# Top-k attention with a SwiGLU block on one core: transposes, scores and sums over V moved between the turns of a software pipeline

## The chip, the core and the metric

The kernel runs on one core of a Trainium2 chip. A core has five engines that run side by side, each with its own queue that it works off in order: TensorE (PE in the profile, PEld for its weight loads), VectorE (DVE), ScalarE (ACT), GpSimd (POOL) and SyncE (SP, which issues most of the DMAs). They wait for each other only through semaphores. TensorE writes into PSUM, from which ScalarE or VectorE copies (evicts) a result into SBUF. The metric is the device time of one execution in microseconds (us).

## What is computed

```python
def _attn_ref(q, k, v):                      # 8 batches, 8 heads, 576 tokens, 64 wide
    scores = scale * np.matmul(q, k.transpose(0, 1, 3, 2))
    kth = np.partition(scores, -top_k, axis=-1)[..., -top_k:-top_k + 1]   # top_k = 32
    scores = np.where(scores >= kth, scores, -1000000000.0)
    attn = np.exp(scores - np.max(scores, axis=-1, keepdims=True))
    attn = attn / (np.sum(attn, axis=-1, keepdims=True) + 1e-09)
    return np.matmul(attn, v).astype(np.float32)

def _moe_ref(x, w_gate, w_val, w_out):       # x is 4608 x 512, w_* 512 x 1536 and 1536 x 512
    g = x @ w_gate
    silu = g * (1.0 / (1.0 + np.exp(-g)))
    return (silu * (x @ w_val) @ w_out).astype(np.float32)
```

The attention's output, with the heads side by side, is the x of the second block. All is float32.

## The kernel before

**Units.** The attention is cut into 160 units: a batch, a tile of 128 queries and a pair of heads. Of the 20 units of a batch, 16 hold two heads of 128 queries ("full" units); the last 4 hold the remaining 64 queries, both heads side by side in one 128-row tile ("J units", `qt == J` in the code), with half the selecting to do. A unit goes through these steps:

- `scores` (line 288): TensorE multiplies Q by K, 4 matmuls into 4 PSUM banks (8 smaller ones for two J units at once); ScalarE evicts them to `sc` (L330, or L315 for J units).
- `select` (333): VectorE finds the 32 largest of each row, four rounds of MAX8 (L347) with three of MATCH_REPLACE8 between (L351), for each head. `shift` (357): GpSimd forms the bias of the exponential (L362).
- `weigh` (367): ScalarE applies Prelu (L374), which sends what is below the 32nd value far down, and exp with a running sum (L379).
- `normalize` (387): VectorE takes the reciprocal of the sum (L392, L393); then ScalarE multiplies head 0 of `e` by it (L397) and GpSimd head 1 (L399; both heads for the first 12 units).
- `turn` (403): TensorE transposes `e` in 128x128 blocks, 9 for a full unit (L412): four that lie in head 0, one that lies across both heads, four in head 1. ScalarE copies them to `et` (L413).
- `values` (423): TensorE sums over V for two units at once, 40 small matmuls in the trace's records for each pair (L448); ScalarE copies the result to `xT` (L465), from which the second block is fed.

PSUM tiles of these steps (`s`, `etps`, `av`, `kqps`) come from one pool of 5 banks, given out in turn; those of the second block from another of 3.

**The second block** (FFN) is cut into blocks of 256 tokens and these into pieces, which the generator `feed` (587) hands out one at a time. A piece is 4 matmuls by `wg` or `wv` (L604; each is two records in the trace), and two pieces make one tile. When a tile is complete, its eviction is put on the list `on_act`: three ScalarE instructions for a `gate` tile (L637 to L639), one for a `value` tile (L644). Each eviction in turn puts a GpSimd multiplication on the list `on_pool` (L640, L645). The product with `w_out` is done in seven "quarters" (`quarter`, 659), in steps of 3 matmuls (L670), with evictions `keep_x`, `keep_y`, `rest_y`, `rest_x` and GpSimd additions and subtractions (L657, L677, L685, L690, L718) between them. `flush` puts the waiting evictions or multiplications into the engine's queue at that place; `piece` (777) flushes a list only when it holds more than one.

**Turns.** The loop at line 870 runs over turns n. In turn n VectorE selects for unit n, ScalarE weighs unit n-1, `normalize(n - 1)` follows late in the turn, and in the middle of the turn TensorE transposes unit n-2 (`TURN = 2`, lines 918 and 919). Every even turn computes the scores of units n+1 and n+2 and the sums over V of units n-4 and n-3, in the order scores, sums, scores; odd turns have none of these. I call a turn with scores and sums *heavy* and one without them *light*. The pieces of the FFN fill the rest of TensorE's turn: `share(n)` (813) credits each turn with a number of pieces, less for the other work of that turn, and `pieces(k)` takes up to k of them at a place if there is credit: two, then one, one, and up to six at the end of the turn.

The order of the work is written out by hand. The last lines (939 to 953) chain every engine's instructions in exactly the order in which the loop issued them, so an instruction that waits holds up all that comes behind it on its engine. While batch b ends, keys and queries of the next batch are transposed (`prep`, 257, in `next(ahead, None)` at lines 922 and 924), one pair of heads in each J turn. In the first turns the FFN's weights are also rounded, on ScalarE, VectorE and GpSimd (`rounded`, 106).

Of the kernel before, what the change touches and what calls it, by code (L numbers as in the profile page):

```python
# [25 lines left out]
def kernel(  # L26
# [43 lines left out]
    NHP = H // 2  # L70
# [6 lines left out]
    AHEAD = 8 * NHP  # L77
# [127 lines left out]
    def rounding(n):  # L205
        for _ in range(n):
            next(weight, None)
# [76 lines left out]
    def n_heads(qt):  # L284

        return 1 if qt == J else 2
# [46 lines left out]
    def select(n):  # L333

        nh = n_heads(units[n][1])
        sc = state[n]["sc"]
        m = small.tile([P, 2, TOP_K], FP32, tag="m", name="m")
        heads = [slice(t * S, (t + 1) * S) for t in range(nh)]
        at = state[n]["at"]
        from_ = [slice(at + t * S, at + (t + 1) * S) for t in range(nh)]  # L340
        e = work.tile([P, 2 * S], FP32, tag="e", name="e", bufs=3)
        state[n] |= dict(m=m, e=e, heads=heads, source=from_)
        cur = sc
        rounds = TOP_K // 8
        for r in range(rounds):
            for t, hs in enumerate(from_):
                nc.vector.max(m[:, t, 8 * r : 8 * r + 8], cur[:, hs])  # L347
                yield
            if r < rounds - 1:
                for t, hs in enumerate(heads):  # L350
                    nc.vector.match_replace(  # L351
                        e[:, hs], m[:, t, 8 * r : 8 * r + 8], cur[:, from_[t]], LOWEST
                    )
                    yield
                cur, from_ = e, heads
# [11 lines left out]
    def weigh(n):  # L367


        st = state[n]  # L370
        sc, m, e, heads, bias = st.pop("sc"), st.pop("m"), st["e"], st["heads"], st.pop("bias")
        tot = small.tile([P, 2], FP32, tag="tot", name="tot")
        for t, (hs, at) in enumerate(zip(heads, st.pop("source"))):
            nc.scalar.activation(  # L374
                e[:, hs], sc[:, at], AF.Prelu, bias=m[:, t, TOP_K - 1 : TOP_K], scale=-1.0,
                alpha=SMALL,
            )
        for t, hs in enumerate(heads):
            nc.scalar.activation(  # L379
                e[:, hs], e[:, hs], AF.Exp, bias=bias[:, t : t + 1], scale=-1.0 / SMALL,  # L380
                accum_out=tot[:, t : t + 1],
            )
        if n < AHEAD:
            nc.scalar.add(tot[:, 0 : len(heads)], tot[:, 0 : len(heads)], EPS)
        st["tot"] = tot

    def normalize(n):
        st = state[n]
        tot, e, heads = st.pop("tot"), st["e"], st.pop("heads")
        nh = len(heads)  # L390
        for t in range(nh if n >= AHEAD else 0):
            nc.vector.tensor_scalar_add(tot[:, t : t + 1], tot[:, t : t + 1], EPS)  # L392
        nc.vector.reciprocal(tot[:, 0:nh], tot[:, 0:nh])  # L393
        yield
        for t, hs in enumerate(heads):
            if t == 0 and n >= 3 * NHP:
                nc.scalar.mul(e[:, hs], e[:, hs], tot[:, t : t + 1])  # L397
            else:
                nc.gpsimd.tensor_tensor(  # L399
                    e[:, hs], e[:, hs], tot[:, t : t + 1].to_broadcast([P, S]), ALU.mult  # L400
                )

    def turn(n):

        last = units[n][1] == J
        e = state[n].pop("e")
        et = work.tile([P, 2 * J + 1, P], FP32, tag="et", name="et")
        for c0, cn in ((0, J), (J, 1)) if last else ((0, J), (J, 1), (J + 1, J)):
            ps = ps_t.tile([P, 512], FP32, tag="t", name="etps")
            for c in range(cn):  # L410
                k0 = S - P if last and c0 == J else (c0 + c) * P
                nc.tensor.transpose(ps[:, c * P : (c + 1) * P], e[:, k0 : k0 + P], ident[:])  # L412
            nc.scalar.copy(  # L413
                et[:, c0 : c0 + cn, :],
                ps[:, 0 : cn * P].rearrange("p (c j) -> p c j", c=cn),
            )
            if c0 == J:
                yield
        state[n]["et"] = et
# [350 lines left out]
    NU = len(units)  # L770
# [6 lines left out]
    def piece():  # L777

        if len(on_act) > 1:
            flush(on_act)  # L780
        if len(on_pool) > 1:
            flush(on_pool)
        for job in early_jobs[:]:
            cost = next(job, 0)
            if cost == 0:
                early_jobs.remove(job)
            elif cost is not None:
                return cost
        if early_jobs:
            return 0  # L790
        while True:
            if not current:
                if not todo or done.get(todo[0], 0) < tokens(todo[0], int(todo[0] >= HALVED)):
                    return 0
                flush(on_act)
                flush(on_pool)
                current.append(feed(todo.pop(0)))
            cost = next(current[0], 0)
            if cost == 0:
                current.pop()  # L800
                continue
            return cost or 0

    def fetch(n):

        b, qt, hp = units[n]
        i = b * NHP + hp
        if qt == 0:
            yield from prep(i)
        if qt == J and i + NHP < len(pairs):  # L810
            load(i + NHP)

    def share(n):


        others = 0.0
        for m, cost in [(m, 0.7) for m in valued(n)] + [(n - TURN, 0.6)]:
            if m >= 0:
                others += cost * (0.5 if units[m][1] == J else 1)
        others += 0.7 * len(scored(n))  # L820
        if units[n + 3][1] == 0:
            others += 0.6

        beside = 5.8 if n < AHEAD else 6.25
        least = 2.0 if n >= 3 * NHP and n % 2 == 0 else 0.0
        return max(least, beside * n_heads(units[n][1]) / 2 - others)

    def scored(n):

        ahead = [n + 1] if n < 2 else [] if n % 2 else [n + 1, n + 2]  # L830
        return [m for m in ahead if m < NU and (units[m][1] < J or m % 2 == 0)]

    def valued(n):

        behind = [] if n % 2 else [n - 4, n - 3]
        return [m for m in behind if 0 <= m < NU]

    def pieces(n):
        for _ in range(n):
            if credit[0] >= 1:  # L840
                credit[0] -= piece()

    def run(steps):
        for _ in steps:
            pass
# [19 lines left out]
    load(2)  # L865
    credit = [0.0]
    no = iter(())
    TURN = 2
    due, steps = [2.0], []
    for n in range(NU + 3):  # L870
        nh = n_heads(units[n][1]) if n < NU else 1
        topk = select(n) if n < NU else no
        norm = normalize(n - 1) if 0 <= n - 1 < NU else no
        nxt = [scores(m) for m in scored(n)]
        ahead = fetch(n + 3 if n else 2) if n + 3 < NU else no

        def dve(k, beside=True):

            for _ in range(k * nh):
                next(topk, None)  # L880
                due[0] += 5 / 6 if beside else 0
                if due[0] >= 1 and not (n == 0 and len(steps) == 5):
                    due[0] -= 1
                    steps.append(n)
                    rounding(1)

        if n >= NU - NHP:
            credit[0] = 8.0
        else:
            credit[0] = min(credit[0] + share(n), share(n) + 1)  # L890
        flush(on_act)
        flush(on_pool)
        if nxt and (n < 2 or len(nxt) > 1):
            run(nxt.pop(0))
        summed = finish_units(valued(n)) if valued(n) else no
        next(summed, None)
        if nxt:
            next(nxt[0])
        early[0]()
        if 0 <= n - 1 < NU:  # L900
            weigh(n - 1)
        run(summed)
        if nxt:
            run(nxt.pop())


        dve(2, beside=False)
        if n == 0:
            run(ahead)
            load(3)  # L910
            ahead = fetch(3)
        if n < NHP:
            load_v(n)
        pieces(2)
        flush(on_act)
        dve(1)
        dve(1)
        if 0 <= n - TURN < NU:
            run(turn(n - TURN))

        flush(on_pool)
        next(ahead, None)
        pieces(1)
        next(ahead, None)
        dve(1)
        pieces(1)
        if n < AHEAD:
            run(topk)
        run(norm)
        run(topk)  # L930
        if n < NU:
            shift(n)
        pieces(6)
# [50 lines left out]
```

## Time and profile before

| | us |
|---|---|
| median of 3 runs | 1712.65 (1712.01 to 1713.51) |
| the profiled execution, its own time | 1712.03 |
| its span in the profile | 1710.2 |
| busy in the span: PE, DVE, ACT, POOL | 1647.4, 1476.5, 1259.5, 799.0 |
| L604, FFN matmuls by wg and wv, busy | 335.9 and 331.4 |
| L412, transposes, busy | 178.2 |
| L325, scores of full units, busy | 169.2 |
| L448, sums over V, busy | 158.0 |

The profile is that of one execution. Its page gives each engine's busy time, the span in 40 slices with the busy tenths of each, the chain of work that ended last, and groups of instructions by source line. Besides the page, the trace answers questions on windows of time (busy time and clock of each engine), on waits (who waited for whom, how long), and as a timeline (instructions in order of time with the idle time before them). In a timeline line the columns are: start, duration, engine, line of the code, operation, output tile and input tiles, shapes, count, and in brackets the idle time before it and what ended that. Matmul records overlap, so the time from the start of one group to the start of the next is the better measure of what a group costs TensorE.

### The profile page before, as it was taken

The page shows a single profiled execution, that of the slowest core. Times are in us where ns is not written, and L with a number is a line of the kernel's source. Part 1 is how long each engine was busy: PE and PEld are TensorE (multiplying, and loading weights), DVE is VectorE, ACT ScalarE, POOL GpSimd, SP SyncE. Part 2 cuts the span into 40 slices and gives each one's busy share as a digit, 9 for nine tenths or more (in the row PEclk, how much of TensorE's full clock was granted, in tenths as well). Part 3 has the DMA queues.
Part 4 walks back from the last instruction along what each step waited for, and adds up shares of the span by engine and source line. Part 5 has one row for each costly group of instructions (what it writes and reads, how often), then busy time and mean ns, then how long its engine had stood idle before and what let it go on. Part 6 is the DMA issues. An engine that isn't in the chain of part 4 may idle for free.

```text
span 1710.2 us, 32128 instructions
## 1 busy us (share of the span) xinstructions
PE 1647.4 (96%) x11600; PEld 1398.2 (82%) x11600; DVE 1476.5 (86%) x3311; ACT 1259.5 (74%) x2901; POOL 799.0 (47%) x914
## 2 busy tenths in 40 slices
PE   5588999999999999999999999999999999999999
PEld 3477698987888887888888888888888888888887
DVE  7999899998989899997999989998999979999400
ACT  7899887877767787768676887777777778676531
POOL 4798545352444425353535334444344433535434
PEclk6699999999999999999999999999999999999999
DMA  7533120003000030001200030000400011000000
GB/s 210 139 112 99 29 72 2 14 1 79 22 13 1 15 86 14 1 8 42 51 14 1 13 74 27 2 13 2 98 1 13 2 44 29 13 2 13 1 13 13
DMA packets 109310, 59.74 MB, mean 35 GB/s; under 512 B 88544, under 2 KB 96992, under 8 KB 109152
## 3 DMA queue, kind: packets, MB, share of 16 engines
q1 hardware_dynamic: 108016, 57.37, 12.9%
q8 instruction: 91, 1.49, 0.4%
q14 instruction: 67, 0.55, 0.1%
q10 hardware_dynamic: 1136, 0.33, 0.1%
HBM read 48.23 MB, written 9.44 MB: 34 GB/s over the span
## 4 chain that ended last, share of the span: by engine, by line
PE 88%; DVE 5%; ACT 4%; DMA 1%; POOL 1%; issue 1%; SPq 0%; POOLq 0%; ACTq 0%
PE f L604 37%; PE x_ps L670 10%; PE av L448 9%; PE s L325 8%; PE y_ps L670 8%; PE etps L412 7%; PE f L517 6%; DVE m L347 2%; DVE e L351 2%; PE kqps L271 1%; PE o_ps L569 1%; PE s L308 1%; ACT e L379 1%; DVE size L124 1%; ACT e L374 0%
## 5 line engine op out<-in xcount | busy, mean ns | idle before, releaser
L347 DVE MAX8 m<-e 128x8 f32<-128x576 f32 x864 | 617.9, 755 | 3.3
L351 DVE MATCH_REPLACE8 e<-m,e 128x576 f32<-128x576 f32 x576 | 425.4, 748 | 0.0
L604 PE MATMUL f<-xT,wg 128*128 128x256 f32 x1440 | 335.9, 382 | 1.3 <-ACT xT L465 1.3
L604 PE MATMUL f<-xT,wv 128*128 128x256 f32 x1440 | 331.4, 380 | 0.0
L604 PEld LDWEIGHTS f<-xT,wg 128*128 128x128 f32 x1440 | 268.9, 190 | 49.0 <-issue 13.1
L604 PEld LDWEIGHTS f<-xT,wv 128*128 128x128 f32 x1440 | 268.2, 190 | 37.5 <-issue 3.8
L640 POOL TENSOR_TENSOR h<-h,half_g 128x512 f32<-128x512 f32 x90 | 114.7, 1275 | 349.2 <-ACT h L639 349.2
L330 ACT ACTIVATE sc<-s 128x288 f32<-128x288 f32 x512 | 170.4, 431 | 105.2 <-PE s L325 104.6
L413 ACT COPY et<-etps 128x512 f32<-128x512 f32 (+1 forms) x448 | 183.6, 486 | 66.0 <-PE etps L412 65.6
L379 ACT ACTIVATE e<-e,bias 128x576 f32<-128x576 f32 x288 | 221.7, 780 | 12.7 <-POOL bias L362 9.7
L374 ACT ACTIVATE e<-sc,m 128x576 f32<-128x576 f32 x288 | 212.3, 792 | 0.6 <-DVE m L347 0.5
L351 DVE MATCH_REPLACE8 e<-m,sc 128x576 f32<-128x576 f32 x288 | 212.6, 748 | 0.0
L412 PE MATMUL etps<-ident,e 128*128 128x128 f32 x1312 | 178.2, 280 | 33.7 <-POOL e L399 15.0
L347 DVE MAX8 m<-sc 128x8 f32<-128x576 f32 x288 | 204.0, 747 | 7.5 <-ACT sc L330 7.5
L412 PEld LDWEIGHTS etps<-ident,e 128*128 128x128 f32 x1312 | 156.2, 144 | 54.7 <-POOL e L399 19.2
L645 POOL TENSOR_TENSOR h<-h,val 128x512 f32<-128x512 f32 x90 | 114.8, 1275 | 155.0 <-ACT val L644 152.4
L325 PE MATMUL s<-kqT 64*128 64x288 f32 x1024 | 169.2, 441 | 13.7 <-ACT sc L330 7.5
L399 POOL TENSOR_TENSOR e<-e,tot 128x576 f32<-128x576 f32 x140 | 161.1, 1154 | 28.5 <-DVE tot L393 28.2
L448 PE MATMUL av<-et,v 128*64 128x128 f32 (+1 forms) x2560 | 158.0, 268 | 0.0
L448 PEld LDWEIGHTS av<-et,v 128*64 128x64 f32 x2560 | 137.7, 140 | 5.9 <-ACT kqT L268 2.7
L325 PEld LDWEIGHTS s<-kqT 64*128 64x128 f32 x1024 | 94.2, 190 | 58.3 <-issue 18.4
L397 ACT ACTIVATE e<-e,tot 128x576 f32<-128x576 f32 x148 | 119.1, 805 | 21.7 <-DVE tot L393 21.6
(86 smaller groups left out, 2249.1 us busy)
## 6 DMA issues: line engine op xcount, KB each, us to landing
v<-in_v_dram SPq DMA_DIRECT2D x32, 256.0 KB, 3.3
kq_in<-in_k_dram SPq DMA_DIRECT2D x63, 128.0 KB, 2.8
kq_in<-in_q_dram SPq DMA_DIRECT2D x63, 128.0 KB, 2.9
w<-in_moe_w_gate_dram SPq DMA_DIRECT2D x12, 512.0 KB, 3.8
w<-in_moe_w_val_dram SPq DMA_DIRECT2D x12, 512.0 KB, 3.8
w<-in_moe_w_out_dram SPq DMA_DIRECT2D x12, 512.0 KB, 3.5
out_dram<-o SPq DMA_DIRECT2D x38, 128.0 KB, 2.4
out_dram<-o SPq DMA_DIRECT2D x16, 256.0 KB, 2.5
```

Of the source, the lines that this page charges most:

```text
L325: nc.tensor.matmul(ps[:, 0:half], slab[d, q0 : q0 + P], slab[d, k0 : k0 + half])
L330: nc.scalar.mul(sc[:, i * half : (i + 1) * half], ps[:, 0:half], scale)
L347: nc.vector.max(m[:, t, 8 * r : 8 * r + 8], cur[:, hs])
L351: nc.vector.match_replace(e[:, hs], m[:, t, 8 * r : 8 * r + 8], cur[:, from_[t]], LOWEST)
L374: nc.scalar.activation(e[:, hs], sc[:, at], AF.Prelu, bias=m[:, t, TOP_K - 1 : TOP_K], scale=-1.0, alpha=SMALL,)
L379: nc.scalar.activation(e[:, hs], e[:, hs], AF.Exp, bias=bias[:, t : t + 1], scale=-1.0 / SMALL, accum_out=tot[:, t : t + 1],)
L399: nc.gpsimd.tensor_tensor(e[:, hs], e[:, hs], tot[:, t : t + 1].to_broadcast([P, S]), ALU.mult)
L412: nc.tensor.transpose(ps[:, c * P : (c + 1) * P], e[:, k0 : k0 + P], ident[:])
L413: nc.scalar.copy(et[:, c0 : c0 + cn, :], ps[:, 0 : cn * P].rearrange("p (c j) -> p c j", c=cn),)
L448: nc.tensor.matmul(av[d, i, 0:ql], weights_, moving, start=c == (0 if last else J), stop=c == (J if last else J - 1),)
L604: nc.tensor.matmul(ps[:, i, :], w[:, kc, m * P : (m + 1) * P], x[:, kc, :], start=(kc == 0), stop=(kc == KC - 1),)
L670: nc.tensor.matmul(ps, lhsT, T[i][m], start=m == 0, stop=m == MQ - 1)
```

## The change

Four things are moved. `TURN` becomes 1: unit n-1 is transposed in turn n, and near the end of it, behind `normalize(n - 1)` and one more place for a piece. `normalize` itself moves one place up. The heavy turns are now the odd ones, with the same two units of scores ahead (n+1 and n+2), and the sums over V take units n-3 and n-2, so each unit leaves the pipeline a turn earlier, and the loop is one turn shorter. `weigh(n - 1)` is issued before the evictions of the scores of unit n+1, behind only the evictions flushed at the top of the turn.

```diff
-        least = 2.0 if n >= 3 * NHP and n % 2 == 0 else 0.0
+        least = 2.0 if n >= 3 * NHP and n % 2 == 1 else 0.0
...
-        ahead = [n + 1] if n < 2 else [] if n % 2 else [n + 1, n + 2]
+        ahead = [n + 1] if n < 3 else [n + 1, n + 2] if n % 2 else []
...
-        behind = [] if n % 2 else [n - 4, n - 3]
+        behind = [n - 3, n - 2] if n % 2 else []
...
-    TURN = 2
+    TURN = 1
     due, steps = [2.0], []
-    for n in range(NU + 3):
+    for n in range(NU + 2):
...
         flush(on_act)
         flush(on_pool)
-        if nxt and (n < 2 or len(nxt) > 1):
+        if 0 <= n - 1 < NU:
+            weigh(n - 1)
+        if nxt and (n < 3 or len(nxt) > 1):
             run(nxt.pop(0))
         summed = finish_units(valued(n)) if valued(n) else no
         next(summed, None)
         if nxt:
             next(nxt[0])
         early[0]()
-        if 0 <= n - 1 < NU:
-            weigh(n - 1)
         run(summed)
         if nxt:
             run(nxt.pop())
...
         dve(1)
         dve(1)
-        if 0 <= n - TURN < NU:
-            run(turn(n - TURN))
-
         flush(on_pool)
         next(ahead, None)
         pieces(1)
         next(ahead, None)
         dve(1)
+        run(norm)
         pieces(1)
-        if n < AHEAD:
-            run(topk)
-        run(norm)
+        if 0 <= n - TURN < NU:
+            run(turn(n - TURN))
         run(topk)
         if n < NU:
             shift(n)
```

No instruction of the computation is added or removed.

## The prediction

> **What bounds the kernel now.** I read the page first, then the windows by stage, TensorE's waits, and two stretches of the timeline.
>
> ```profile
> PE 1647.4 (96%) x11600; PEld 1398.2 (82%) x11600; DVE 1476.5 (86%) x3311; ACT 1259.5 (74%) x2901; POOL 799.0 (47%) x914
> ...
> PE   5588999999999999999999999999999999999999
> ...
> PEclk6699999999999999999999999999999999999999
> ```
>
> TensorE is idle in the first four slices and nearly nowhere else. The windows (engines' busy us in order PE, PEld, DVE, ACT, POOL, then clock) say it in numbers:
>
> ```profile
> 60.00:80.00 20.00, 11.51 (x66) 8.73 (x66) 20.00 (x43) 18.02 (x42) 15.35 (x14) 0.50 0.39 110
> ...
> 800.00:1000.00 200.00, 200.00 (x1380) 169.38 (x1379) 182.02 (x417) 149.72 (x345) 84.15 (x100) 1.00 0.10 24
> ```
>
> Early VectorE has no gap; from about 200 us (VectorE's turn 17) TensorE has none. Added up, TensorE idles 50.5 us before 200 us, 6.7 from there to 1620, and 5.6 after. TensorE's waits between 170 and 1640 us are small change (us in total, times, longest):
>
> ```profile
> PE s L325 <- ACT et L413: 2.0, 3, 1.0
> PE etps L412 <- ACT e L397: 1.7, 1, 1.7
> PE f L604 <- ACT xT L465: 1.3, 1, 1.3
> ```
>
> Is "busy" full speed? 16 records of L604 follow each other 3.46 us apart at 905.85 to 909.31 us, and just as far at 1595.60 to 1599.06, when VectorE is mostly idle. So time is TensorE's work plus its idle time, and the work does not change. The skill speaks against this reading: the Trainium skill, "Perfetto Trace Analysis", section "Identifying the Most-Contended Engine", calls matmul busy time a bad measure of nearness to the limit and would have weight loads used, 82% here. Were the other 18% room to absorb waits, the loss below would largely vanish; the equal spacing says there is none.
>
> **The change, part by part.**
>
> *Start.* At the end of turn 17 the new order has TensorE ahead by one unit's transposes (0.98), two units' sums (2.34), one unit's scores (1.17) and one piece (1.8): 6.3 us of work done in time that VectorE sets. That is the most that can be gained: **-6.3**. ScalarE, 17 to 20 us busy in each 20 us there, could eat it if its queue now waits for late transposes: at half a us in each of the first 14 turns, 7 us the other way. I take the gain, as VectorE's row there is full and ScalarE's is not.
>
> *Middle.* Before, a unit is normalized in one turn and transposed in the next. Here is a heavy turn before the change:
>
> ```profile
> 900.14 1.24 PE L325 MATMUL s<-kqT 64*128 64x288 f32 x8
> 901.31 3.72 PE L604 MATMUL f<-xT,wv 128*128 128x256 f32 x16
> ...
> 902.59 0.17 DVE L393 RECIPROCAL tot<-tot 128x2 f32<-128x2 f32 x1
> ...
> 904.87 1.15 PE L412 MATMUL etps<-ident,e 128*128 128x128 f32 x9
> 905.07 0.59 ACT L644 COPY val<-f 128x512 f32<-128x512 f32 x1 [1.22 <-PE f L604]
> ...
> 905.80 1.27 POOL L645 TENSOR_TENSOR h<-h,val 128x512 f32<-128x512 f32 x1 [6.10 <-ACT val L644]
> ...
> 907.02 1.15 POOL L399 TENSOR_TENSOR e<-e,tot 128x576 f32<-128x576 f32 x1
> ...
> 909.31 1.15 PE L412 MATMUL etps<-ident,e 128*128 128x128 f32 x9
> ```
>
> The second scores end at 901.31. Head 1's multiplication ends at 908.17, 6.86 us later, because it stands in GpSimd's queue behind the tile's own. TensorE needs it at 909.75, in the next turn, 1.6 us to spare. The change puts these transposes behind three pieces of the same turn: 3 x 1.73 + 0.44 (four transposes of head 0) = 5.63 us after the second scores, 1.2 us before the result. Nothing covers that; the queue behind it (FFN, scores) waits along. Over 39 heavy turns of the trace the same distance is 3.5 to 9.4 us, 6.3 on average.
>
> I walked the new order of turns 101 to 120 (a batch) by hand, with these distances to the next start: scores 1.17, sums 2.34, piece 1.73, quarter step 1.29, transposes 0.98 (J unit 0.55); evictions: gate 1.48, value 0.48, scores 1.17 (first of four 0.43); Prelu and exp 2.85 (J unit 1.43); 0.6 from there to the reciprocal's end; L397 0.81, L399 1.15, GpSimd's h 1.2 to 1.27; 0.8 from the end of transposes to their last copy; 0.1 to 0.2 a signal. Waits that result:
>
> - *Transposes in heavy turns.* If the turn's first two pieces complete a tile, its eviction and multiplication stand ahead of L397 and L399. Value: L399 done 6.7 after the second scores (the row: 6.86), a wait of 1.2. Gate: 7.7, in all 2.1. With only two pieces in the turn: 2.9. If the tile was begun earlier, 0 to 0.4. The eight heavy turns: 0.4, 1.2, 1.2, 0, 2.1, 0.4, 2.9, 0 = 8.2.
> - *Second scores.* They take the four banks of the first scores (5 banks: 4 and one for the sums). These evictions now stand behind `weigh`, and that behind what is flushed at the top. TensorE needs the first bank 3.51 after its turn begins. With a tile that completes just at the turn's end, ScalarE gives it at 0.2 + 1.48 + 2.85 + 0.43 = 4.96: a wait of 1.5. Turns 103, 105, 113, 119: 6.0; elsewhere ScalarE is early enough.
> - *Transposes in light turns*, after four pieces (6.92): copies of the last transposes 0.8, a pending value 0.48, `weigh` 2.85, the gate tile 1.48, its multiplication, then L399: ready at 8.15 against 7.36. Six turns: 0.85, 0.3, 0.65, 0, 0.85, 0.35 = 3.0.
> - *Quarters.* In turns 108 and 116 GpSimd has three additions (0.73, 0.73, 1.26) and three L718 (2.1) ahead of L399, all behind `keep_y` at 4.6: ready 10.7, needed 5.6. Twice 5.1 = 10.2.
> - *J units with `prep`.* L397 stands behind the copies of `prep`, and the transposes come right after `prep`'s own:
>
> ```profile
> 820.25 0.27 PE L264 MATMUL kqps<-ident,kq_last 128*128 128x128 f32 x1
> ...
> 820.45 0.58 ACT L276 COPY kqT<-kqps 128x512 f32<-128x512 f32 x1 [1.47 <-PE kqps L271]
> ...
> 821.20 0.80 ACT L397 ACTIVATE e<-e,tot 128x576 f32<-128x576 f32 x1
> ...
> 823.82 0.71 PE L412 MATMUL etps<-ident,e 128*128 128x128 f32 x5
> ```
>
> From 820.36 (end of L264's slot) to 822.00 is 1.6; before, a product of 3.46 lies between. Turns 117 to 119: 1.7 each, 120: 0.4; 5.5.
>
> Sum: 32.9 us in 20 turns. Turns 64 to 81, walked the same way, give 28.9 in 18. I drop waits under 0.5 us, which the walk can't resolve (1.85 and 1.75): 31.1 / 20 and 27.2 / 18, together 1.53 a turn. TensorE is the bound in turns 17 to 157, 141 turns: **+216**. VectorE needs 10.2 us a full turn (1570.23 to 1580.43) where TensorE now has 10.7 plus 1.5, so VectorE is no new bound; its 65.6 us of waits for exp become longer or move, at no cost.
>
> *Tail.* Before, the last units' chain leaves TensorE idle for 1.78 us, and the clock falls to 0.78 to 0.87 for a few us (16 records take 4.25 instead of 3.46): some 3.6 lost. After, units 158 and 159 each pass Prelu, exp, reciprocal, L397, transposes and copy in turn with no pieces beside: 9.9 us to the first product, 3.7 of it work, and a clock drop of 2.5: 8.7. **+5**.
>
> Register moves, SP's queue and DMAs: the stores follow their evictions, and `load_v` comes a turn earlier; queues are far from full (q1 12.9%). Nothing.
>
> Sum against the execution's own 1712.0: 1712.0 - 6.3 + 216 + 5 = **1927**. The median of the runs is 0.6 us above that execution, which I ignore.
>
> **Rivals.**
>
> *A, all these waits are real:* 1927, as above.
>
> *B, only what single rows show is real:* heavy transposes (8.2) and J units (5.5), 13.7 a batch or 0.69 a turn: 97, so 1712 - 6 + 97 + 5 = 1808. It holds if ScalarE reaches `weigh` well before TensorE ends its turn, so that second scores and light turns find all ready, and if quarters seldom meet the transposes. For it: ScalarE is idle a quarter of the time. Against it: it waits for TensorE, not for want of work.
>
> *C, the clock falls too.* After the idle 1.78 us at 1641 the clock read 0.87 and 0.78; after 1.75 us at 394 it stayed 1.00. So it depends. Two waits of 5 us a batch at the tail's 1.8 lost each add 25; if waits in 3 of 8 turns do it, 1.8 x 3 / 8 x 141 turns is 95. So 1950 to 2020. The Trainium skill, "TensorE: Matmul & The Clock Gate", section "Why this matters for your kernels", warns only of gaps above some 3 us; by it the two long ones alone would cost.
>
> *D, the shorter pipeline pays.* Its place is the first 200 us, its price 6.3: 1712.0 - 6.3 = 1706. It decides if the middle's waits sum to less than 6 us, 0.04 a turn, that is if the normalized unit is always there first, as with the 1.6 us to spare above, and the tail is hidden. For it: `weigh` and `normalize` both move up. Against: 6.86 against 5.63.
>
> That the change does not do what it says is out: the built order has unit n-1 transposed behind `normalize(n - 1)` in the same turn on all engines. "First" for Prelu and exp is not quite so: pending evictions stay ahead.
>
> **How the numbers follow.** A and what lies between A and B, 0.64; B 0.18; C beyond 2000, 0.10; D 0.06; within 0.2% of before 0.02 (0.2% is about what a measurement can tell from no change). The range 1780 to 2000 takes in B (1808) and the milder C, and leaves out 0.18. Faster 0.06, same 0.02, slower 0.92.
>
> **What would show it.** In the profile after: TensorE's busy tenths fall to 8 or so through the middle; `PE etps L412` waiting for POOL e L399 or ACT e L397 leads TensorE's waits with 80 us or more; `PE s L325` waits for ACT sc L330, some 40; `DVE tot L392` still waits for exp. Wrong would be: TensorE still without gaps from 200 to 1600 us (D), waits of L412 without those of L325 (B), or a clock under 0.95 in the middle (C).

## The result, and the profile after

The changed kernel takes 2029.4 us, the median of 5 runs (2028.1 to 2030.9), against 1713.1 us before in the same session: 1.1845 times as long, 95% interval 1.1828 to 1.1863. The direction and the waits were forecast, the size was not: 1927 was predicted, with 2000 as the upper end. The profiled execution after has a span of 2027.6 us, 317.4 more than before.

The page after (busy time, then the busy tenths in 40 slices):

```profile
PE 1742.0 (86%) x11600; PEld 1449.8 (72%) x11600; DVE 1476.8 (73%) x3311; ACT 1287.7 (64%) x2901; POOL 797.1 (39%) x914
...
PE   4667989898989888988898989989798988898989
...
PEclk6778999999999999999999999999999999899999
```

TensorE's row has 8s and 9s (and one 7) where it had only 9s. VectorE does the same work, which is now 73% of a longer span. The windows (PE, PEld, DVE, ACT, POOL, then the clock) show the loss all along, and a clock below 1.00 where it was 1.00:

```profile
0.00:200.00 200.00, 122.58 (x830) 101.06 (x831) 143.67 (x315) 143.91 (x317) 125.16 (x120) 0.74 0.41 117
...
800.00:1000.00 200.00, 178.24 (x1184) 147.35 (x1181) 159.10 (x360) 130.99 (x300) 68.84 (x83) 0.97 0.10 25
```

TensorE's waits between 230 and 1900 us (us in total, times, longest); before, all of TensorE's waits there came to some 7 us:

```profile
PE etps L412 <- POOL e L399: 102.0, 77, 4.9
PE etps L412 <- ACT e L397: 65.2, 53, 5.4
PE s L325 <- ACT sc L330: 23.9, 22, 2.3
```

This is the list that the prediction named: transposes wait for the two normalizing multiplications, second scores for ScalarE's evictions. A heavy turn after, to be held against the one before:

```profile
1121.64 3.72 PE L604 MATMUL f<-xT,wg 128*128 128x256 f32 x16
...
1125.40 0.60 ACT L637 ACTIVATE h<-f 128x512 f32<-128x512 f32 x1 [2.35 <-PE f L604]
...
1126.89 0.77 ACT L397 ACTIVATE e<-e,tot 128x576 f32<-128x576 f32 x1
1127.08 1.27 POOL L640 TENSOR_TENSOR h<-h,half_g 128x512 f32<-128x512 f32 x1 [2.61 <-ACT h L639]
1127.72 0.66 PE L412 MATMUL etps<-ident,e 128*128 128x128 f32 x4 [0.63 <-ACT e L397]
1128.30 1.15 POOL L399 TENSOR_TENSOR e<-e,tot 128x576 f32<-128x576 f32 x1
...
1129.51 0.77 PE L412 MATMUL etps<-ident,e 128*128 128x128 f32 x5 [1.13 <-POOL e L399]
```

Here the first two pieces complete a gate tile. Its eviction (1125.40) stands ahead of head 0's multiplication (1126.89), its own multiplication on GpSimd (1127.08) ahead of head 1's (1128.30). TensorE, done with its third piece, waits 0.63 us and then 1.13 us.

To see where the time goes, I read from both traces when VectorE forms the reciprocal of each unit, and cut the run at units 19 and 155. Unit 19's comes at 231.0 us before and 278.4 after: **47.4 us later**. From there to unit 155's it takes 1357.0 us before and 1632.4 after: **275.4 us more**. The rest is 5.5 us shorter: TensorE has 51 records of L604 fewer left by then, about six pieces or 11 us, which it has done in the middle instead. The middle holds 188 us of idle TensorE time in 152 waits (5.6 in 7 before), and TensorE is slowed by its clock there: busy time in the stretches at half clock, times the missing half, is 47 us (none before).

### The profile page after: what moved, and what is told of

Same layout as the page of the kernel before. It is cut to its first block, busy times and chain, and to the rows that moved or that the text cites. A ratio compares the mean times of both kernels' runs of the same rounds, so it can differ in the third digit from the quotient of the medians.

```text
span 2027.6 us, 32166 instructions
## 1 busy us (share of the span) xinstructions
PE 1742.0 (86%) x11600; PEld 1449.8 (72%) x11600; DVE 1476.8 (73%) x3311; ACT 1287.7 (64%) x2901; POOL 797.1 (39%) x914
## 4 chain that ended last, share of the span: by engine, by line
PE 51%; ACT 17%; POOL 17%; issue 12%; DVE 2%; SPq 0%; DMA 0%; POOLq 0%; ACTq 0%; DVEq 0%
PE f L604 18%; PE x_ps L670 8%; PE etps L412 6%; PE av L448 5%; POOL e L399 5%; PE s L325 5%; ACT e L379 4%; PE y_ps L670 3%; POOL h L640 3%; PE f L517 3%; ACT et L413 3%; POOL h L645 2%; ACT e L374 2%; POOL h L718 1%; POOL p L657 1%
## 5 line engine op out<-in xcount | busy, mean ns | idle before, releaser
L413 ACT COPY et<-etps 128x512 f32<-128x512 f32 (+1 forms) x448 | 200.4, 474 | 371.5 <-PE etps L412 371.2
L412 PE MATMUL etps<-ident,e 128*128 128x128 f32 x1312 | 216.0, 302 | 246.9 <-POOL e L399 175.3
L412 PEld LDWEIGHTS etps<-ident,e 128*128 128x128 f32 x1312 | 160.9, 152 | 303.8 <-POOL e L399 203.5
L604 PE MATMUL f<-xT,wg 128*128 128x256 f32 x1440 | 337.3, 384 | 0.0
L604 PE MATMUL f<-xT,wv 128*128 128x256 f32 x1440 | 334.9, 383 | 0.0
L604 PEld LDWEIGHTS f<-xT,wv 128*128 128x128 f32 x1440 | 271.7, 191 | 42.6 <-issue 7.1
L604 PEld LDWEIGHTS f<-xT,wg 128*128 128x128 f32 x1440 | 269.2, 191 | 45.8 <-issue 11.9
L392 DVE TENSOR_SCALAR tot<-tot 128x1 f32<-128x1 f32 x228 | 32.5, 151 | 345.6 <-ACT e L379 345.2
L351 DVE MATCH_REPLACE8 e<-m,sc 128x576 f32<-128x576 f32 x288 | 211.9, 742 | 0.0
L325 PE MATMUL s<-kqT 64*128 64x288 f32 x1024 | 180.1, 450 | 26.0 <-ACT sc L330 24.5
L399 POOL TENSOR_TENSOR e<-e,tot 128x576 f32<-128x576 f32 x140 | 160.6, 1151 | 26.7 <-DVE tot L393 26.7
L448 PE MATMUL av<-et,v 128*64 128x128 f32 (+1 forms) x2560 | 163.2, 273 | 0.0
L325 PEld LDWEIGHTS s<-kqT 64*128 64x128 f32 x1024 | 107.8, 192 | 67.1 <-ACT sc L330 32.5
L448 PEld LDWEIGHTS av<-et,v 128*64 128x64 f32 x2560 | 143.0, 144 | 6.0 <-issue 3.0
```

The source lines that it names most:

```text
L325: nc.tensor.matmul(ps[:, 0:half], slab[d, q0 : q0 + P], slab[d, k0 : k0 + half])
L351: nc.vector.match_replace(e[:, hs], m[:, t, 8 * r : 8 * r + 8], cur[:, from_[t]], LOWEST)
L399: nc.gpsimd.tensor_tensor(e[:, hs], e[:, hs], tot[:, t : t + 1].to_broadcast([P, S]), ALU.mult)
L413: nc.scalar.copy(et[:, c0 : c0 + cn, :], ps[:, 0 : cn * P].rearrange("p (c j) -> p c j", c=cn),)
L448: nc.tensor.matmul(av[d, i, 0:ql], weights_, moving, start=c == (0 if last else J), stop=c == (J if last else J - 1),)
L604: nc.tensor.matmul(ps[:, i, :], w[:, kc, m * P : (m + 1) * P], x[:, kc, :], start=(kc == 0), stop=(kc == KC - 1),)
```

## Experiments

The two columns on the right are the same two stages, against the kernel before: how much later unit 19's reciprocal comes, and how much longer it is from there to unit 155's, both in the profiled execution. Runs 1 to 4, 8 and 9 are one execution each; the others are medians of four or more. The four of run 10 lie up to 9 us apart, so a few us between single executions mean nothing.

| run | time, us | start | middle |
|---|---|---|---|
| before (profiled) | 1712.0 | 0 | 0 |
| after | 2029.4 | 47.4 | 275.4 |
| 1: GpSimd's flush behind normalize | 1947.4 | 30.0 | 211.9 |
| 2: Prelu and exp back | 1991.1 | 48.9 | 235.6 |
| 3: prep's second half behind normalize | 2005.5 | 45.0 | 253.9 |
| 4: transposes at the top of the next turn | 1999.2 | 24.9 | 266.2 |
| 5: before, Prelu and exp first | 1771.8 | 15.7 | 43.8 |
| 6: before, Prelu and exp first, normalize up | 1770.9 | 15.1 | 45.3 |
| 7: after, extra matmuls in long gaps | 2008.6 | 45.5 | 254.8 |
| 8: 1, 2 and 3 together | 1889.9 | 30.6 | 154.2 |
| 9: 1 and 4 together | 1929.4 | 15.1 | 207.5 |
| 10: normalize ahead of all pieces | 1841.6 | 15.7 | 116.4 |
| 11: 10 and 2 together | 1826.2 | 16.9 | 100.9 |

Two theories were put against each other. *Queue theory*: each wait is made by what stands ahead of the unit's own instruction in ScalarE's or GpSimd's queue. *Chain theory*: Prelu, exp, reciprocal, multiplication and transposes of a unit are too long for one turn in any order, so that taking one obstacle away only moves the wait. (Head 0 and head 1 below stand for the multiplications of the two heads, L397 on ScalarE and L399 on GpSimd.)

**1. GpSimd's flush behind normalize.**

```diff
-        flush(on_pool)
         next(ahead, None)
         pieces(1)
         next(ahead, None)
         dve(1)
         run(norm)
+        flush(on_pool)
```

> The kernel after, with the flush of GpSimd's waiting multiplications put behind normalize, so that head 1's multiplication no longer stands behind the tile's own multiplication or the quarter's additions and subtractions. Queue theory (each wait is made by what stands ahead of the unit's own instruction in ScalarE's or GpSimd's queue): TensorE's 102 us of waits for that multiplication between 230 and 1900 us fall below 25, the ten gaps of 4.6 us go, and with them most of the stretches at half clock: 1910 to 1950 us. Rival (the unit's own chain of Prelu, exp, reciprocal and multiplication is too long for one turn, whatever the order): the waits move to head 0's multiplication on ScalarE and the time stays above 1990 us.

1947.4 us. TensorE's waits in the middle (240 to 1800 us):

```profile
PE etps L412 <- ACT e L397: 61.6, 50, 5.4
PE etps L412 <- POOL e L399: 57.4, 17, 4.9
```

Sixty of the 77 waits for head 1 are gone, and head 0's did not grow: the queue theory holds for them. One point was missed: the waits for head 1 fall to 57.4 us and not below 25, since the ten long gaps stay, 46 us of them, because the quarter's additions and subtractions are issued inside `feed`, which this edit does not move.

**2. Prelu and exp behind the evictions of the first scores again.**

```diff
-        if 0 <= n - 1 < NU:
-            weigh(n - 1)
         if nxt and (n < 3 or len(nxt) > 1):
             run(nxt.pop(0))
...
         early[0]()
+        if 0 <= n - 1 < NU:
+            weigh(n - 1)
         run(summed)
```

> The kernel after, with Prelu and exp issued behind the evictions of the first scores again, as before the change. Queue theory: the 24 us of waits of the second scores go and nothing else changes in the middle; the start (turn 19's reciprocal 47 us later than before the change) stays within 10 us, since it is held up by the copies of the transposes: 1995 to 2010 us. Rival for the start (Prelu and exp placed first make ScalarE wait for VectorE and GpSimd): turn 19 comes 25 us or more earlier, 1960 to 1980 us.

1991.1 us, somewhat better than expected. The second scores no longer wait for ScalarE, and the middle is 39.8 us shorter, more than the 24 us on record as their wait: 21 us of idle time are gone there, and with them 8 us of clock. The start does not move (48.9 against 47.4), so in this kernel Prelu and exp placed first are not what delays it.

**3. prep's second half behind normalize.**

```diff
         next(ahead, None)
         pieces(1)
-        next(ahead, None)
         dve(1)
         run(norm)
+        next(ahead, None)
         pieces(1)
```

> The kernel after, with the second half of the keys' and queries' transposes (prep) put behind normalize, so that head 0's multiplication stands ahead of prep's last copies. Queue theory: of the 1.6 to 1.7 us that TensorE waits in each of 28 turns with prep about 1.0 goes: 1995 to 2008 us. Rival (chain too long): 2020 to 2030 us.

2005.5 us. The waits for head 0 fall from 71.3 to 50.2 us over the whole run: in those turns head 0's multiplication was held up by prep's copies.

**4. Transposes at the top of the next turn.**

```diff
         if 0 <= n - 1 < NU:
             weigh(n - 1)
+        if 0 <= n - 2 < NU:
+            run(turn(n - 2))
...
-        if 0 <= n - TURN < NU:
-            run(turn(n - TURN))
         run(topk)
```

> The kernel after, with a unit's transposes moved from the end of its turn to the top of the next turn, behind Prelu and exp and ahead of the scores. TensorE gains cover only in light turns (one or two pieces), ScalarE's Prelu and exp no longer stand behind the copies of the transposes. Queue theory: at the start VectorE's waits for the rounding (48 us for size from ScalarE's L117) fall by more than half and turn 19 comes 25 to 40 us earlier; in the middle the light turns' waits and the long gaps in them go, those of heavy turns and of turns with prep stay: 1900 to 1955 us. Rival for the start (it is TensorE's late transposes themselves, or Prelu placed first, not the copies in ScalarE's queue): turn 19 moves by less than 10 us.

1999.2 us: half right. The start comes 22.5 us earlier, as VectorE's wait for the rounding falls from 48.0 to 22.5 us: the copies in ScalarE's queue are one cause of the late start. The middle was missed by some 60 us. The waits of the whole run say where the gain went:

```profile
PE etps L412 <- POOL e L399: 90.3, 56, 10.9
PE s L325 <- ACT et L413: 71.7, 46, 3.3
```

The transposes wait less, and the scores now wait for the transposes' PSUM banks, whose copies stand behind Prelu and exp. I had forgotten that the copies hold three of the five banks that the scores need.

**5. The kernel before, with Prelu and exp first.** The same lines as in 2, the other way round, in the kernel before.

> The kernel before, with one part of the change alone: Prelu and exp issued ahead of the evictions of the first scores. Queue theory: second scores wait in about half of the heavy turns, 0.5 to 1.5 us each, 20 to 45 us; transposes still have their slack; the start is later by 0 to 10 us: 1730 to 1765 us. Rival (placed first it lets VectorE's reciprocal come earlier and costs nothing): 1708 to 1716 us.

1771.8 us, 1.0337 times the kernel before (1.0322 to 1.0353), a little over the range. So this part of the change costs 57 us even where the transposes have slack: 43.8 in the middle, where the walk had six us in 20 turns or 42, and 15.7 at the start, where I had allowed 10. TensorE's largest wait in the whole run (us in total, times, longest):

```profile
PE s L325 <- ACT sc L330: 60.6, 26, 9.4
```

**6. The change without its shorter pipeline.** As 5, with normalize one place up and its special case for the first 32 turns removed.

```diff
         dve(1)
+        run(norm)
         pieces(1)
-        if n < AHEAD:
-            run(topk)
-        run(norm)
```

> The kernel before, with Prelu and exp first and normalize one place up, that is the change without its shorter pipeline: transposes stay two turns behind, in the middle of the turn, scores and sums stay at even turns. Queue theory: within 10 us of the run with Prelu and exp first alone, 1725 to 1765 us, so that some 270 us of the change's 316 belong to the transposes' new place. Rival: normalize placed earlier blocks the evictions behind it, 1780 us or more.

1770.9 us: as 5. Normalize's place costs nothing by itself in the longer pipeline. The other 258 us, whatever the parts do to each other included, come with the transposes' new place, the heavy turns at odd turns and the sums a turn earlier, which depend on one another and were not tried one by one.

**7. Extra work in the long gaps.** In turns in which L718 was issued ahead:

```diff
             ps = ps_t.tile([P, 512], FP32, tag="t", name="etps")
+            for _ in range(12 if held[0] and c0 == J and not last else 0):
+                nc.tensor.matmul(ps[:, 0:P], ident[:], ident[:])
```

> The kernel after, with 12 matmuls of the identity (2.7 us of extra work, overwritten by the transposes that follow) ahead of the transpose across both heads, only in turns in which the quarter's subtractions (L718) were issued ahead of it. Clock theory (gaps above some 2.3 us drop the clock to half for 4 to 6 us, shorter ones don't): the extra work lies in gaps of 4.6 us, which shrink below 2 us, and the half clock behind them goes: about 10 times 2.5 us, 1998 to 2012 us in spite of the added work. Rival (the clock falls with the sum of idle time, or the gaps cost only their length): 2026 to 2035 us.

2008.6 us (2005.9 to 2010.7): more work, 21 us less time. A long gap in the kernel after, and the clock behind it:

```profile
1110.75 1.33 PE L412 MATMUL etps<-ident,e 128*128 128x128 f32 x5 [4.56 <-POOL e L399]
...
1111.87 2.57 PE L670 MATMUL x_ps<-t,h 128*128 128x256 f32 x6
```

```profile
1111.00:1114.00 3.00, 3.00 (x10) 2.56 (x10) 3.00 (x7) 2.15 (x5) 0.73 (x1) 0.50 0.00 0
```

The same place with the extra matmuls (the lines of the code have moved: L411 the extra ones, L414 the transposes, L673 the quarter):

```profile
1094.60 2.85 PE L411 MATMUL etps<-ident 128*128 128x128 f32 x24
...
1099.34 0.77 PE L414 MATMUL etps<-ident,e 128*128 128x128 f32 x5 [1.89 <-POOL e L399]
...
1099.94 1.46 PE L673 MATMUL x_ps<-t,h 128*128 128x256 f32 x6
```

The gap is 1.89 instead of 4.56 us, and six matmul records behind it take 1.46 instead of 2.57 us. The time lost to the clock in the middle falls from 47 to 27 us. This shows what the long gaps cost; it does not test the expectation's limit of 2.3 us, which the traces contradict (see the last section).

**8. Three orders together.** Edits 1, 2 and 3.

> The kernel after, with three orders changed together: Prelu and exp behind the first scores' evictions, GpSimd's flush behind normalize, prep's second half behind normalize. Queue theory: the three gains add, since they lie in different turns or places: 2029 less about 95, 25 and 27, so 1865 to 1905 us. Rival (chain too long): less than half of that, above 1960 us.

1889.9 us. In the middle the three alone save 63.5, 39.8 and 21.5, together 124.8; in one kernel they save 121.2. They add, as separate queue orders should.

**9. Edits 1 and 4 together, for the start.**

> The transposes at the top of the next turn behind Prelu and exp, together with GpSimd's flush behind normalize. For the start: against the kernel before, turn 19's reciprocal was 47 us late in the kernel after, 25 with the transposes' copies behind Prelu and exp, 30 with the flush behind normalize. Queue theory: these are two orders in two queues, ScalarE's and GpSimd's, and add: turn 19 is 0 to 15 us late. Rival (one cause seen twice): 20 to 25 us late. Whole time 1910 to 1950 us, since the wait of the first scores for the transposes' copies (72 us) stays.

1929.4 us, turn 19 at 15.1 us: at the edge between the theories. Up to unit 15 the two edits save 17.4 and 29.2 of 45.3 us, together 36.8, so they overlap in part. About 8 us up to unit 15 and 15 up to unit 19 stay unexplained.

**10. Normalize ahead of all pieces.**

```diff
-        pieces(2)
-        flush(on_act)
         dve(1)
         dve(1)
+        dve(1)
+        run(norm)
+        pieces(2)
+        flush(on_act)
         flush(on_pool)
         next(ahead, None)
         pieces(1)
         next(ahead, None)
-        dve(1)
-        run(norm)
         pieces(1)
```

> The kernel after, with normalize (reciprocal and both multiplications) issued ahead of the turn's first pieces instead of behind three of them, so that the multiplications wait for nothing but the unit's own chain: no tile's eviction, h, quarter or prep copies ahead. Queue theory: TensorE's waits for the transposes' data fall from 247 us to below 70 (mostly before 200 us), the clock in the middle stays at 1.00 but for a few places; what remains is Prelu and exp placed first (40 to 57 us by two other runs) and 20 to 35 us at the start: 1770 to 1825 us. Rival (the chain is too long for one turn): above 1860 us.

1841.6 us, 1.0748 times the kernel before (1.0724 to 1.0772). 188 us are back, but it misses the range by 17. The waits of the middle:

```profile
PE s L325 <- ACT sc L330: 22.7, 20, 2.3
PE etps L412 <- ACT e L397: 17.0, 15, 5.4
PE x_ps L670 <- POOL xT L677: 16.2, 5, 3.9
PE x_ps L670 <- POOL h L718: 14.6, 9, 2.8
```

Head 1's multiplication is waited for no more. So for most units the chain fits one turn, and the queue theory is right for most of the loss. The first line is the wait of the second scores, which this edit does not touch. The last two are new or have grown (L677 from 2.4 us): head 1's multiplication now stands in GpSimd's queue, waiting for its reciprocal (256 us in 96 waits between 240 and 1750 us), ahead of the subtractions that the quarters need.

**11. Edits 10 and 2 together.**

> As the run with normalize ahead of the pieces, and Prelu and exp behind the evictions of the first scores again. Queue theory: 40 to 57 us less than that run, 1725 to 1775 us: the pipeline one turn shorter costs little once nothing foreign stands ahead of the chain, and what is left is the start. Rival (chain too long): above 1820 us.

1826.2 us, 1.0660 times the kernel before (1.0641 to 1.0679): 51 above the queue theory's range, and in the rival's (above 1820). Moving Prelu and exp back, worth 39.8 us in the middle in run 2, is worth 15.5 here. The middle's 101 us hold 60 of added idle TensorE time, nearly all in waits for head 0 (26.2) and for L677, L718 and L690 (41), and 22 of clock. The second group is again an order in GpSimd's queue. What is left for head 0 may be the chain theory's share; I did not test it, so that part stays open. No version here beats the kernel before, and none of these runs points to one.

## Why the prediction was wrong

*What bounds the kernel: right.* TensorE's idle time and clock carry the loss, and VectorE is no new bound: its waits for exp rise from 101 to 345 us (L392, whole run), and no wait of TensorE is put down to it. (The prediction's 65.6 us for them was misread: on the page that is ScalarE's wait for the transposes, L413. No term of the sum rests on it.) The equal spacing of matmuls was the right sign that there was no room in TensorE, and the doubt drawn from the Trainium skill, "Perfetto Trace Analysis", section "Identifying the Most-Contended Engine", did not bear out: the added idle time went through to the span.

*Start: the step that failed, in sign.* "I take the gain, as VectorE's row there is full and ScalarE's is not": -6.3 predicted, +47.4 measured. The trace after shows a loop through four engines:

```profile
91.92 2.24 POOL L399 TENSOR_TENSOR e<-e,tot 128x576 f32<-128x576 f32 x2
93.12 2.44 PE L412 MATMUL etps<-ident,e 128*128 128x128 f32 x9 [5.04 <-POOL e L399]
...
95.59 0.59 ACT L413 COPY et<-etps 128x512 f32<-128x512 f32 x1 [0.56 <-PE etps L412]
...
96.07 1.44 ACT L374 ACTIVATE e<-sc,m 128x576 f32<-128x576 f32 x2
...
99.17 0.66 ACT L117 ACTIVATE size<-w 128x512 f32<-128x512 f32 x1
...
99.93 0.43 DVE L124 TENSOR_SCALAR size<-size 128x512 int32<-128x512 int32 x1 [7.71 <-ACT size L117]
```

GpSimd ends the multiplication at 94.16, TensorE transposes at a slow clock, ScalarE copies, then does Prelu and exp, and only then the next weight rounding (L117), for which VectorE has waited 7.71 us. Between 20 and 200 us VectorE waits 48.0 us for L117; in the whole run before it was 4.0. VectorE's full row was the sum of a schedule in which ScalarE, 85 to 99% busy between 20 and 180 us, was nearly a bound too; the copies' new place let it idle 34.4 us in that time, waiting for transposes (0.9 before). I had named this at half a us a turn; it was 3 us a turn over 15 turns. Run 4 gives back 22.5 us by that one order, run 9 32 by two. The last 15 us stay open: run 5 loses as much by Prelu and exp placed first, but in run 11 these are back and unit 19 is still 16.9 us late.

*Waits in the middle: right in kind and, in total, nearly in size.* Walked: 216 us. Measured: 182 us more idle time on record, in 145 more waits. The records understate a wait: a matmul's record outlasts its slot (eight records take 1.89 us on record and follow at 1.73), by which I estimate that about 25 more belong to the waits. The total agrees better than its parts, so some of it is luck. The parts, in us, walked (turns 101 to 120, scaled to 141 turns) and on record in the middle:

| | walked | on record |
|---|---|---|
| transposes in heavy turns | 52 | 45 |
| transposes in light turns | 17 | 36 |
| quarters (on record: the eleven gaps above 4 us) | 72 | 52 |
| J units | 36 | 29 |
| second scores | 42 | 24 |

Runs 2 and 5 put the second scores at 39.8 and 43.8, but with 8 and 10 us of clock in it, which the walk did not have. Single cases: a quarter ahead of head 1, walked 5.1, measured 4.56; the gate case, walked 2.1 in all, in the turn shown 0.63 + 1.13.

*Clock: wrong, and the second term that failed.* The forecast had none of it in the middle. Rival C priced the long gaps at 25 us and the worse case at 95, but only 0.10 went to more than 2000. Measured: 47, in 22 stretches at half clock. All eleven waits above 4 us have one beside them, but so have shorter ones:

```profile
853.04 1.65 PE L325 MATMUL s<-kqT 64*128 64x288 f32 x8 [1.32 <-ACT sc L330]
854.62 5.41 PE L604 MATMUL f<-xT,wv 128*128 128x256 f32 x16
```

After a wait of 1.32 us, 16 records take 5.41 us instead of the 3.72 at 1121.64; seven other waits of 1.32 us had no such effect. So the 1.78 us in the tail, behind which the clock had fallen, was a fair sign, and the step that failed was to leave it out of the sum because "it depends". Run 7 shows cause and price for the long gaps: about 20 us for ten.

*Tail: about right.* +5 was predicted. From unit 155 on it is 5.5 us less, but with some 11 us of TensorE's work gone from there to the middle; so the tail itself costs about 5 us more.

*The sum:* 1712 + 47 (start) + 182 + 25 (waits) + 47 (clock) + 10.5 (work moved into the middle, all lines together) - 5.5 (the rest) = 2018, 11 short of the measured time, which I cannot assign.

*Rivals.* D's mechanism (the shorter pipeline does more work early) is there, six pieces done before unit 155 instead of after it, but it has no place to pay: in the middle TensorE is the bound, and the start, where it would have paid, became longer. B was too mild: second scores, light turns and quarters are as real as the rest.

## What to carry to other kernels

Shortening a software pipeline by a turn is not free for the bound engine: look up in the trace how long before its use each operand is ready (here 1.6 us), and compare it with how far the use is moved. Then walk the queues of the engines that make the operand, since a wait is made by what stands ahead in an in-order queue, and moving one order can pass the wait to the next queue (runs 4 and 10). And a stage whose bound engine is full is not safe if a second engine is 90% busy there: a wait put into that one's queue comes out as the stage's length.

## What the runs showed of the hardware

The granted clock in these traces is 1.00 or 0.50, and it changes only on a grid of 3.41 us: the 22 halved stretches in the middle of the kernel after last 3.41 or 6.83 us each. What goes with a halved stretch is TensorE's idle time within the 3.41 us just before it, and not the length of one gap. Over the middles of all thirteen traces, none of the 5112 full-clock stretches with less than 1.3 us of idle time on record was followed by a halved one, and all 129 with more than 2.2 us were; of the 282 between, 67 were. So a wait of 2.46 us (at 797.33), which the grid splits into 1.8 and 0.7 us, left the clock at 1.00, while one of 1.32 us within one stretch (at 853.04) halved it. What decides between 1.3 and 2.2 us stays open.

The Trainium skill, "TensorE: Matmul & The Clock Gate", section "Why this matters for your kernels", warns of gaps above about 3 us; here shorter ones were enough, so a design that counts on 3 us is too near the edge. And useless matmuls in a gap can pay: some 2.7 us of them in each of ten such gaps made the kernel 21 us faster (run 7).
